# A state-space layer and a gated feed-forward on one Trainium2 core: three steps moved in a hand-ordered kernel

## The chip, the cores and the metric

The kernel runs on one core of one Trainium2 chip. The metric is the device time of one execution in microseconds (us). The time before is the median of five runs: 128.35 us, lowest 126.94, highest 129.66. The profile shown here was taken from one execution of its own.

A core has a matrix engine (TensorE, PE in the profile; PEld is its weight load), a vector engine (VectorE, DVE), an activation engine (ScalarE, ACT), a general engine (GpSimd, POOL) and a queue engine (SyncE, SP) that issues most transfers. Matrix products land in PSUM, in banks; DVE and ACT read PSUM, POOL works on SBUF only.

## The reference

Two layers follow each other. The first is a chunked linear recurrence (a state-space layer) over 4 batches, 8 heads and 768 tokens, with head size 32 and state size 16. The second is a feed-forward with a gate, on 3072 tokens of width 256.

```python
# attention-like layer, per chunk of 32 tokens
cum = np.cumsum(log(a))                       # per head
L   = exp(cum_i - cum_j), causal
M   = (C @ B.T) * L
y   = M @ x + (C @ state) * exp(cum)
state = exp(sum(log a)) * state + sum_j (B_j x_j) * exp(cum_last - cum_j)
# feed-forward
gate = np.maximum(y @ w_gate, 0.0)            # 256 -> 1536
val  = y @ w_val                              # 256 -> 1536
out  = (gate * val) @ w_out                   # 1536 -> 256
```

## The kernel before

**Tiles.** The 3072 tokens are worked in 12 pairs of 256 tokens (pairs 0 to 11, three to a batch) and in 6 blocks of 512 tokens for the feed-forward. Block b takes pairs 2b and 2b+1. `yT` holds the first layer's result, turned, as 128 partitions by 2 halves (k) by 3072 tokens.

**One pair of the first layer** goes through these steps:

- `load(p)`: B, C and x come from memory, six transfers on SP's queue for pairs 4 and later (lines 120 and 121).
- `scale(p, ...)`: POOL multiplies B and C by decay factors into a token tile `tok` (line 333, four operations), issues the transposing transfer `turn_dma` on SP's queue (line 294, the result is `turned`), and casts x into `xb` (line 348). It stands in the queue of POOL and in that of SP where it is called.
- `G`: eight small products of `turned` into four banks (line 540). `gevac`: ACT copies two of the banks (lines 559, 562), POOL blanks their upper triangle (`causal`, line 548), DVE does the others (lines 565, 567).
- `sums`: products of `tok` and `xb` give the state sums (line 593); `states` spreads them on DVE (line 606); `inter` multiplies the carried state with `turned` (line 624).
- `Dm`: sixteen products of the masked `gs` with `xb` (line 635); `yevac` copies the result to `yT` (line 648).

Pairs 0 to 3 have forms of their own ("wide"): `gcopy` and `gmask` for the masks (lines 432, 428), `adds`, `carry` (DVE, line 472) and `pass_on` (ACT, line 481) for the states, `inter_wide` and `D_wide` (lines 493, 518), and `yevac_wide`, whose two halves go to ACT and DVE (line 532).

**The feed-forward of a block** has 12 slices f. `gv(b, f)` makes gate and value for 512 tokens (lines 660, 663), ACT takes the positive part (line 666) and DVE multiplies (line 667) into `h`. `gvh(b, f, u)` does the same for half the tokens (u = 0 or 1; lines 678, 681, 684), so that the first pair of a block can start before the second is ready. With `later=True` it returns the DVE product as a function (`finish`), to be called where the program wants it. `fout` and `foevac` make the block's output and copy it out (lines 705, 721 and others); the transfer out is issued on SP's queue.

**Order.** There is no planner. The order on each engine is the order in which the program writes its steps, and `in_order` at the end keeps it. What waits is decided by semaphores between the queues. `bank()` hands out five shared PSUM banks in turn, so a product into a bank also waits until the bank's last reader is done.

Of the kernel before, what the change touches and what calls it, by code (L numbers as in the profile page):

```python
# [29 lines left out]
def kernel(  # L30
# [13 lines left out]
    nc = tc.nc  # L44
# [8 lines left out]
    NPAIR = T // 256  # L53
# [12 lines left out]
    def bank(name="bank", shape=(128, 512), dtype=FP32):  # L66
        return mm.tile(list(shape), dtype, tag="shared", bufs=NSHARED, name=name)
# [204 lines left out]
    def inverse(b0, b1):  # L272
        for b in range(b0, b1):
            nc.vector.reciprocal(scaleBC[:, b, :, 0, :], scaleBC[:, b, :, 1, :])
# [4 lines left out]
    def scale(p, eng, ceng):  # L279
        scale_bc(p, eng)  # L280
        cast_x(p, ceng)
# [142 lines left out]
    def gmask(p, q, eng, psum=False):  # L424
        s = st[p]
        d = s["gw"][:, q]
        m = (wmask if p < FIRST else wmask3).unsqueeze(2).to_broadcast([128, 2, 2, 128])
        eng.tensor_tensor(out=d, in0=s["gp"][q] if psum else d, in1=m, op=ALU.mult)  # L428
# [47 lines left out]
    def pass_on(p, i):  # L476

        c = 2 * p + i
        S[c + 1] = m = att.tile([128, 2, D], BF16, tag="Sw", name="Sw", bufs=3)
        src = st[p]["A"][i] if c == 0 else T_[c]  # L480
        nc.scalar.mul(m.rearrange("s t d -> s (t d)"), src, dec[:, c:c + 1])
# [28 lines left out]
    def D_wide(p, qs=(0, 1, 2, 3)):  # L510
        s = st[p]
        for t in range(2):
            for r in range(2):
                for i in range(2):
                    half = slice(64 * i, 64 * i + 64)
                    y = s["yw"][i][:, 0:256].rearrange("s (t m) -> s t m", t=2)
                    for q in qs:
                        nc.tensor.matmul(
                            out=y[32 * q:32 * q + 32, t],
                            lhsT=s["xb"][half, 4 * t + q, r], rhs=s["gw"][half, q, r, t],  # L520
                            start=not s["begun"][i] and t == 0 and r == 0, stop=True,
                            tile_position=(64 * i, 32 * q), skip_group_check=True)

    def yevac_wide(p, *engs):
        s = st[p]
        for i, eng in enumerate(engs):
            dst = yT[:, :, p * 256 + i * 128:p * 256 + (i + 1) * 128]
            src = s["yw"][i][:, 0:256].rearrange("s (t m) -> s t m", t=2)
            if p >= FIRST:
                dst = dst.rearrange("s t (m r) -> s t r m", r=2)  # L530
                src = src.rearrange("s t (r m) -> s t r m", r=2)
            (eng.copy if eng is nc.scalar else eng.tensor_copy)(out=dst, in_=src)  # L532
# [158 lines left out]
    def fout(b, ts, fs=range(NF)):  # L691
        if fs[0] == 0 and (ts % 2 == 0 or b == NBLK - 1):
            fst["o"] = bank("o", (128, 2, DM))
        o = fst["o"]
        if b == NBLK - 1 and ts == 3:
            fst["oh"] = [o[:, 1, 0:128], bank("o", (128, 128))]
            for i, oh in enumerate(fst["oh"]):
                for f in range(NF):
                    nc.tensor.matmul(
                        out=oh, lhsT=fst[b][:, f, ts * 128:(ts + 1) * 128],  # L700
                        rhs=wo[:, f, i * 128:(i + 1) * 128], start=(f == 0),
                        stop=(f == NF - 1), skip_group_check=True)
            return
        for f in fs:
            nc.tensor.matmul(  # L705
                out=o[:, ts % 2], lhsT=fst[b][:, f, ts * 128:(ts + 1) * 128],
                rhs=wo[:, f], start=(f == 0), stop=(f == NF - 1),
                skip_group_check=True)

    def foevac(b, ts):  # L710
        last = b == NBLK - 1
        if ts % 2 == 0 and not last:
            if ts and not b:
                fst["ob"] = ob = ffn.tile([128, 2, DM], FP32, tag="ob", name="ob", bufs=3)
                nc.scalar.copy(out=ob[:, 0], in_=fst["o"][:, 0])
            return
        if 1 <= b <= 3:
            if ts == 1:
                fst["ob4"] = ffn.tile([128, 4, DM], FP32, tag="ob4", name="ob4")
            ob = fst["ob4"]  # L720
            nc.scalar.copy(out=ob[:, ts - 1:ts + 1], in_=fst["o"])
            if ts == 3:
                nc.sync.dma_start(
                    out=out[b * 512:(b + 1) * 512, :].rearrange("(i p) m -> p i m", p=128),
                    in_=ob)
            return
        ob = fst.pop("ob", None) or ffn.tile([128, 2, DM], FP32, tag="ob", name="ob", bufs=3)
        r0 = b * 512 + ts * 128
        if last and ts == 3:
            for i, (eng, q) in enumerate(((nc.scalar.copy, nc.scalar),  # L730
                                          (nc.vector.tensor_copy, nc.sync))):
                cs = slice(i * 128, (i + 1) * 128)
                eng(out=ob[:, 1, cs], in_=fst["oh"][i])
                q.dma_start(out=out[r0:r0 + 128, cs], in_=ob[:, 1, cs])
            return
        if last:
            i = ts % 2
            (nc.vector.tensor_copy if i else nc.scalar.copy)(out=ob[:, i], in_=fst["o"][:, i])
            (nc.sync if i else nc.scalar).dma_start(out=out[r0:r0 + 128, :], in_=ob[:, i])
            return  # L740
        if b == 0 and ts == 3:
            nc.scalar.copy(out=ob[:, 1], in_=fst["o"][:, 1])
        else:
            nc.scalar.copy(out=ob, in_=fst["o"])
        nc.sync.dma_start(
            out=out[r0 - 128:r0 + 128, :].rearrange("(i p) m -> p i m", p=128), in_=ob)
# [6 lines left out]
    V, A_, P_ = nc.vector, nc.scalar, nc.gpsimd  # L753
# [54 lines left out]
    def halves(b, u, *fs):  # L808
        for f in fs:
            gvh(b, f, u)  # L810
# [14 lines left out]
    late = [gvh(0, f, 0, True) for f in (1, 2, 3)]  # L825
# [52 lines left out]
    gcopy(2, 1)  # L878
    gmask(2, 3, V, True)
    gmask(2, 0, V)  # L880
    gmask(2, 1, V)
    fout(0, 1)
    foevac(0, 1)
    adds(2)
    carry(2, 0)
    pass_on(2, 0)
    fout(0, 2)
    foevac(0, 2)
    inter_wide(2)
# [10 lines left out]
    gmask(3, 3, V, True)  # L900
    states(3)
    gmask(3, 1, V)
    halves(1, 0, 0, 1, 2, 3, 4)
    y_wide(3)
    inter_full(3, 1)
    D_wide(3)
    yevac_wide(3, A_, V)
    halves(1, 0, 5)

    for b in range(1, NBLK):  # L910
        P, Q, W = 2 * b + 2, 2 * b + 3, 2 * b + 1
        more = P < NPAIR
        for n in (P + 2, P + 3):
            if n < NPAIR and b > 1:
                load(n)

        def at(name, *fs):

            return more and f == fs[min(b, len(fs) - 1)]

        n = 6 if b == 1 else 4
        if b > 1:
            for f in range(n):
                gvh(b, f, 0)
                if f == 1:
                    inter(W, 0)
                    inter(W, 1)
                    Dm(W)
                    if more:
                        sums(P)  # L930
                    yevac(W, nc.scalar)
                    if more:
                        states(P)
        for f in range(n):
            gvh(b, f, 1)
        for f in range(n, NF):
            gv(b, f)
            if b == 1 and at("scale P", 99, 6):
                scale(P, nc.gpsimd, nc.gpsimd)
                load(P + 2)  # L940
                inverse(2, 4)
            if at("scale Q", 9, 6, 4):
                scale(Q, nc.gpsimd, nc.gpsimd)
                if b == 1:
                    load(P + 3)
            if at("scale next P", 11, 11, 9) and P + 2 < NPAIR:
                scale(P + 2, nc.gpsimd, nc.gpsimd)
        if more:
            inter(P, 0)
            if b > 1:  # L950
                inter(P, 1)
        fout(b, 0)
        foevac(b, 0)
        if more:
            G(P)
            if b == 1:
                sums(P)
            gevac(P)
            if b == 1:
                states(P)  # L960
        fout(b, 1)
        foevac(b, 1)
        fout(b, 2)
        foevac(b, 2)
        if more:
            if b == 1:
                inter(P, 1)
            Dm(P)
            sums(Q)
            yevac(P, nc.scalar)  # L970
            G(Q)
            gevac(Q)
            states(Q)
        fout(b, 3)
        foevac(b, 3)

    in_order(tc)

# [29 lines left out]
```

## Time and profile before

| | |
|---|---|
| time, median of 5 runs | 128.35 us (126.94 to 129.66) |
| the profiled execution | 126.94 us |
| its span, first to last instruction | 125.2 us |
| PE busy | 117.8 us (94%) |
| DVE busy | 88.3 us (71%) |
| ACT busy | 76.3 us (61%) |
| POOL busy | 47.9 us (38%) |
| mean granted TensorE clock | 0.997 |

The span leaves 1.74 us of the profiled execution's time outside it. Busy shares are means over the whole span and say little on one stage. Where an engine stood still, and who released it, is read from its waits and its rows in order of time. A row of the timeline gives start, duration, engine, line, operation, tiles and count, and in brackets the idle time before it with the releaser. `SPq` rows are the time that SP took to issue a transfer; when the data had arrived is told by the DMA view ("us to landing", counted from the issue).

### The profile page before, as it was taken

The page shows a single profiled execution, that of the slowest core. Times are in us where ns is not written, and L with a number is a line of the kernel's source. Part 1 is how long each engine was busy: PE and PEld are TensorE (multiplying, and loading weights), DVE is VectorE, ACT ScalarE, POOL GpSimd, SP SyncE. Part 2 cuts the span into 40 slices and gives each one's busy share as a digit, 9 for nine tenths or more (in the row PEclk, how much of TensorE's full clock was granted, in tenths as well). Part 3 has the DMA queues.
Part 4 walks back from the last instruction along what each step waited for, and adds up shares of the span by engine and source line. Part 5 has one row for each costly group of instructions (what it writes and reads, how often), then busy time and mean ns, then how long its engine had stood idle before and what let it go on. Part 6 is the DMA issues. An engine that isn't in the chain of part 4 may idle for free.

```text
span 125.2 us, 3656 instructions
## 1 busy us (share of the span) xinstructions
PE 117.8 (94%) x1398; PEld 82.4 (66%) x1404; DVE 88.3 (71%) x199; ACT 76.3 (61%) x168; POOL 47.9 (38%) x108
## 2 busy tenths in 40 slices
PE   6989999999969996999999999999999999999990
PEld 6766784576756476784467874477864677844790
DVE  4798989771969963698854987845997855687510
ACT  0558598755948631687634786736786545876420
POOL 6499918980364217450333712311800033000000
PEclk9999999999999999999999999999999999999998
DMA  3999999967899999895998099993390002200022
GB/s 66 224 197 141 168 185 196 181 125 102 95 122 185 177 115 110 106 255 72 119 114 166 31 218 113 110 88 86 135 100 0 0 0 89 84 0 0 0 89 84
DMA packets 77489, 13.93 MB, mean 111 GB/s; under 512 B 70064, under 2 KB 77472, under 8 KB 77472
## 3 DMA queue, kind: packets, MB, share of 16 engines
q1 hardware_dynamic: 70128, 10.61, 55.0%
q0 software_dynamic: 4288, 2.36, 14.0%
q10 hardware_dynamic: 3056, 0.72, 2.6%
q8 instruction: 11, 0.18, 0.6%
q14 instruction: 6, 0.05, 0.1%
HBM read 11.13 MB, written 3.15 MB: 114 GB/s over the span
## 4 chain that ended last, share of the span: by engine, by line
PE 68%; SPq 11%; DMA 8%; POOL 6%; issue 2%; DVE 1%; ACT 0%; POOLq 0%; DVEq 0%
PE o L705 17%; PE gv L678 16%; PE val L663 12%; PE gate L660 11%; SPq L120 6%; DMA xr<-in_x_dram 6%; SPq L121 3%; PE y L635 2%; DMA bcr<-in_C_dram 2%; PE w L184 2%; SPq L89 2%; POOL wg L194 2%; PE g L540 2%; POOL bs L317 1%; PE y L624 1%
## 5 line engine op out<-in xcount | busy, mean ns | idle before, releaser
L667 DVE TENSOR_TENSOR h<-r,val 128x512 bf16<-128x512 bf16 x44 | 30.0, 685 | 7.3 <-ACT r L666 7.2
L705 PE MATMUL o<-wo,h 128*128 128x256 bf16 x276 | 33.1, 273 | 0.0
L666 ACT ACTIVATE r<-gate 128x512 bf16<-128x512 f32 x44 | 26.3, 597 | 9.7 <-PE gate L660 9.3
L705 PEld LDWEIGHTS <-h 128*128 128x128 bf16 x276 | 25.9, 98 | 5.3 <-issue 1.7
L663 PE MATMUL val<-yT,wv 128*128 128x512 bf16 x88 | 26.2, 379 | 0.3
L684 DVE TENSOR_TENSOR h<-r,gv 128x256 bf16<-128x256 bf16 x56 | 22.7, 419 | 3.6 <-ACT r L681 2.8
L660 PE MATMUL gate<-yT,wg 128*128 128x512 bf16 x82 | 24.9, 379 | 0.0
L681 ACT ACTIVATE r<-gv 128x256 bf16<-128x256 f32 x56 | 21.2, 385 | 3.6 <-PE gv L678 1.6
L678 PE MATMUL gv<-yT,wg 128*128 128x256 bf16 x112 | 21.6, 273 | 1.3 <-DVE yT L532 1.3
L678 PE MATMUL gv<-yT,wv 128*128 128x256 bf16 x112 | 21.4, 273 | 0.0
L333 POOL TENSOR_TENSOR tok<-bcr,scaleBC 128x128 bf16<-128x128 f32 x32 | 12.1, 402 | 20.7 <-DMA bcr<-in_B_dram 18.7
L565 DVE TENSOR_TENSOR gs<-g,maskUT 128x512 bf16<-128x512 f32 x16 | 10.3, 686 | 12.6 <-issue 5.2
L548 POOL TENSOR_SCALAR_AFFINE_SELECT gs<-gs 128x512 bf16<-128x512 bf16 (+1 forms) x16 | 7.9, 520 | 27.3 <-ACT gs L559 27.3
L663 PEld LDWEIGHTS <-wv 128*128 128x128 bf16 x88 | 8.6, 98 | 10.4
L660 PEld LDWEIGHTS <-wg 128*128 128x128 bf16 x88 | 8.5, 98 | 8.9
L678 PEld LDWEIGHTS <-wg 128*128 128x128 bf16 x112 | 10.3, 98 | 3.1 <-DVE yT L532 1.5
L678 PEld LDWEIGHTS <-wv 128*128 128x128 bf16 x112 | 11.0, 98 | 1.3
L559 ACT CAST gs<-g 128x512 bf16<-128x512 f32 x8 | 4.7, 589 | 6.7 <-PE g L540 6.7
L648 ACT CAST yT<-y 128x512 bf16<-128x512 f32 x8 | 4.7, 585 | 6.4 <-PE A_ps L593 3.7
L428 DVE TENSOR_TENSOR gs<-g,wmask 128x512 bf16<-128x512 f32 x9 | 5.9, 681 | 2.6 <-PE g L413 2.6
L184 PE MATMUL w<-warm 128*128 128x128 bf16 x49 | 5.3, 276 | 1.1 <-DVE tmask L158 1.1
L184 PEld LDWEIGHTS <-warm 128*128 128x128 bf16 x58 | 4.8, 123 | 1.7 <-DVE tmask L158 1.1
(121 smaller groups left out, 116.1 us busy)
## 6 DMA issues: line engine op xcount, KB each, us to landing
xr<-in_x_dram SPq DMA_DIRECT2D x17, 128.0 KB, 3.2
out_dram<-ob SPq DMA_DIRECT2D x3, 512.0 KB, 4.8
bcr<-in_C_dram SPq DMA_DIRECT2D x17, 64.0 KB, 2.9
bcr<-in_B_dram SPq DMA_DIRECT2D x17, 64.0 KB, 3.1
out_dram<-ob SPq DMA_DIRECT2D x4, 256.0 KB, 2.4
xr<-in_x_dram SPq DMA_DIRECT2D x3, 256.0 KB, 3.9
wo<-in_moe_w_out_dram POOLq DMA_DIRECT2D x2, 384.0 KB, 9.1
wg<-in_moe_w_gate_dram POOLq DMA_DIRECT2D x4, 128.0 KB, 4.4
```

Of the source, the lines that this page charges most:

```text
L184: nc.tensor.matmul(out=w, lhsT=warm, rhs=rhs, start=True, stop=True)
L333: eng.tensor_tensor(out=dst[:, t, j * (1 + t)], in0=src[:, j, :, t], in1=f[:, j, :, 4 * t:4 * t + 4].to_broadcast([128, 2, 4, N]), op=ALU. ...
L548: nc.gpsimd.affine_select(out=dst, in_=dst, pattern=[[0, n], [1, 128]], compare_op=ALU.is_ge, fill=0.0, base=0, channel_multiplier=-1)
L565: nc.vector.tensor_tensor(out=d[:, q], in0=g[q], in1=m, op=ALU.mult)
L660: nc.tensor.matmul(out=g, lhsT=wg[:, k, fs], rhs=yT[:, k, tk], start=(k == 0), stop=(k == 1))
L663: nc.tensor.matmul(out=v, lhsT=wv[:, k, fs], rhs=yT[:, k, tk], start=(k == 0), stop=(k == 1))
L666: nc.scalar.activation(r, g, AF.Relu)
L667: nc.vector.tensor_tensor(out=fst[b][:, f], in0=r, in1=v, op=ALU.mult)
L678: nc.tensor.matmul(out=gv_[:, j], lhsT=w[:, k, fs], rhs=yT[:, k, tk], start=(k == 0), stop=(k == 1), skip_group_check=True)
L681: nc.scalar.activation(r, gv_[:, 0], AF.Relu)
L684: nc.vector.tensor_tensor(out=fst[b][:, f, u * 256:(u + 1) * 256], in0=r, in1=gv_[:, 1], op=ALU.mult)
L705: nc.tensor.matmul(out=o[:, ts % 2], lhsT=fst[b][:, f, ts * 128:(ts + 1) * 128], rhs=wo[:, f], start=(f == 0), stop=(f == NF - 1), skip_gr ...
```

## The change

Three steps are moved; nothing is added to or taken from the computation, and the matrix engine's list of instructions keeps its order.

```diff
     gmask(2, 0, V)
-    gmask(2, 1, V)
     fout(0, 1)
-    foevac(0, 1)
     adds(2)
     carry(2, 0)
     pass_on(2, 0)
+    foevac(0, 1)
+    gmask(2, 1, V)
     fout(0, 2)
...
     gmask(3, 1, V)
-    halves(1, 0, 0, 1, 2, 3, 4)
+    late = [gvh(1, f, 0, True) for f in range(5)]
+    late[0]()
     y_wide(3)
     inter_full(3, 1)
     D_wide(3)
+    late[1]()
     yevac_wide(3, A_, V)
+    for fin in late[2:]:
+        fin()
     halves(1, 0, 5)
...
-            if at("scale next P", 11, 11, 9) and P + 2 < NPAIR:
+            if at("scale next P", 99, 99, 9) and P + 2 < NPAIR:
                 scale(P + 2, nc.gpsimd, nc.gpsimd)
...
         fout(b, 3)
         foevac(b, 3)
+        if b == 1:
+            scale(P + 2, nc.gpsimd, nc.gpsimd)
```

- Pair 2: on DVE `carry` goes ahead of the mask of bank 1; on ACT `pass_on` goes ahead of the copy of `fout(0, 1)`.
- Pair 3: DVE's half of `yevac_wide` comes after two of the first five half-tile products instead of after all five.
- Pair 6: in block 1 (P = 4) its `scale` moves from slice f = 11 to the end of the block. On POOL it is now behind the four `causal` operations of pairs 4 and 5; on SP its transposing transfer is now behind block 1's transfer out.

## The prediction

> **What bounds the kernel now.** I first read the totals and the chain that ended last, then the waits of PE.
>
> ```profile
> PE 117.8 (94%) x1398; PEld 82.4 (66%) x1404; DVE 88.3 (71%) x199; ACT 76.3 (61%) x168; POOL 47.9 (38%) x108
> PE 68%; SPq 11%; DMA 8%; POOL 6%; issue 2%; DVE 1%; ACT 0%; POOLq 0%; DVEq 0%
> ...
> PE gv L678 <- DVE yT L532: 1.3, 1, 1.3
> PE y L635 <- POOL gs L548: 1.0, 1, 1.0
> ```
>
> PE sets the time, yet the chain has 11% in SP's issuing and 8% in transfers: between 21 and 49 us it runs along SP's queue. After the start PE has two stalls worth naming, the last two lines, and the change aims at both. Since PE keeps its order, the question is who is next to hold it once they are gone. For that I read the rows in order of time.
>
> First place, 33 to 44 us:
>
> ```profile
> 33.55 1.73 DVE L684 TENSOR_TENSOR h<-r,gv 128x256 bf16<-128x256 bf16 x5
> 35.20 0.43 DVE L532 CAST yT<-y 128x256 bf16<-128x256 f32 x1
> ...
> 34.22 0.44 ACT L532 CAST yT<-y 128x256 bf16<-128x256 f32 x1
> ...
> 35.69 0.28 PE L678 MATMUL gv<-yT,wg 128*128 128x256 bf16 x1 [1.33 <-DVE yT L532]
> ...
> 39.62 1.28 SPq L294 DMA_TRANSPOSE turned<-tok  x1
> ...
> 43.68 0.25 PEld L624 LDWEIGHTS <-Sm 128*128 128x128 bf16 x2 [0.18 <-DMA turned<-tok]
> 43.83 0.28 PE L624 MATMUL y<-turned,Sm 128*128 128x128 bf16 x2
> ```
>
> PE waits 1.33 us for DVE's half of pair 3, which stands behind five products. Eight us later the weight load of `inter(4, 0)` waits 0.18 us for the transposed pair 4: that transfer lands just as PE comes.
>
> Second place, 48 to 54 us (the first two rows are the same work on pair 4, standing for its undisturbed length):
>
> ```profile
> 34.84 1.48 POOL L333 TENSOR_TENSOR tok<-bcr,scaleBC 128x128 bf16<-128x128 f32 x4 [1.50 <-DMA bcr<-in_B_dram]
> 36.26 0.61 POOL L348 CAST xb<-xr 128x512 bf16<-128x512 f32 x1
> ...
> 48.65 0.61 POOL L348 CAST xb<-xr 128x512 bf16<-128x512 f32 x1 [0.65 <-DMA xr<-in_x_dram]
> 49.22 1.00 POOL L548 TENSOR_SCALAR_AFFINE_SELECT gs<-gs 128x512 bf16<-128x512 bf16 x2
> 49.91 0.65 PE L635 MATMUL y<-gs,xb 128*32 128x128 bf16 x16 [0.95 <-POOL gs L548]
> 50.55 0.40 PE L540 MATMUL g<-turned 32*128 32x256 bf16 x8
> 51.74 0.99 POOL L548 TENSOR_SCALAR_AFFINE_SELECT gs<-gs 128x512 bf16<-128x512 bf16 x2 [1.53 <-ACT gs L559]
> 53.62 0.26 PE L593 MATMUL A_ps<-xb,tok 128*32 128x64 bf16 x12
> ```
>
> POOL holds pair 4's blanking back until pair 6's x has come and is cast; `Dm(4)` waits. Then pair 5, and at 53.62 `sums(6)`, the first reader of what `scale(6)` makes. In this execution `scale(6)` was done at 49.26, 4.4 us ahead.
>
> **The change, part by part.** All times are on the axis of the profiled execution: span 125.2 us, 1.74 around it, 126.94 in all. That is 1.41 under the median, so the difference found is carried to the median of 128.35.
>
> *Pair 2's carry.* DVE does the two remaining masks in 1.00 us from 26.93, the carry from 27.85 (0.27); ACT passes the state on from 28.16 (0.35), and PE takes it at 28.54. One mask less ahead (about 0.46) brings the state to about 28.05. But PE comes at 28.54 behind the twelve products of `fout(0, 2)` (27.13 to 28.61), so the gain is between 0 and the 0.2 us that its weight load waited for ACT; I take 0. The mask that moves back ends near 28.2, and `D_wide(2)` starts at 28.87: 0.6 us of cover. The output copy on ACT moves from 27.06 to about 28.1; its transfer is issued only at 38.44, behind a backlog on SP. If either cover failed it would cost its shortfall, some tenths, which part two's idle time on PE would swallow.
>
> *Pair 3's evacuation.* The last mask ends at 33.62. The five products take 1.73, so with 0.42 each they follow at (1.73 − 0.42)/4 = 0.33. Two end at 34.30. PE's `D_wide(3)` ends at 34.15, and on pair 2 DVE's copy began 0.13 after that end (29.29 to 29.42); so it starts at 34.30 and ends at 34.73 by its own 0.43. ACT's half ends at 34.66. Release took 0.06 before (35.63 to 35.69): PE resumes at 34.79, not 35.69. Saved: 0.90. The three products left end at 34.73 + 1.04 = 35.8; PE needs the banks they free from 35.5 on, one each 0.44 us, in order, and the first of them is free at 35.1. So DVE makes no new wait.
>
> PE then reaches `inter(4, 0)` at 42.9, and there stands the transposed pair 4. Its issue starts at 39.62, and the DMA view gives for it:
>
> ```profile
> turned<-tok SPq DMA_TRANSPOSE x1, 4.0
> ```
>
> It lands at 43.62. The weight load follows at 43.68 whatever PE did before. SP is busy without a break from 28.7 to 45.5 with loads that nothing moved here, so the issue at 39.62 stays. The 0.90 us become idle time between 42.9 and 43.8: kept, 0 to 0.9; I take 0, because two views (the wait and the landing) agree within 0.1.
>
> The Trainium skill, page "Perfetto Trace Analysis", section "Summary: the profiler window per engine type", states that for a transfer issued in hardware the shown window ends with the issue and hides the data movement. The issue row here is 1.28 us and the landing 4.0. By the row taken as the transfer's end (40.90) the 0.90 would be kept and the sum would be about 126.1; by the landing it would not. The trace's own landing decides, and it speaks against this edit.
>
> *Pair 6's scale.* Without it POOL blanks pair 4 as soon as ACT's two copies are there (45.77 and 46.25, ending 46.63): done by about 47.4. `Dm(4)` can follow `inter(4, 1)` at 48.79. Sixteen products take 0.33 and the eight of `sums(5)` 0.1, so `G(5)` could start at 49.24, against 50.55: saved 1.31. `G(5)` needs the transposed pair 5, issued at 45.56, 3.7 to landing: 49.26, plus about 0.14 as above for pair 4: 49.40. So 1.15.
>
> Now the work moved is late. From `G(5)` to POOL's start on pair 5 it was 51.74 − 50.55 = 1.19; ACT's copy of pair 4 stands between as before, block 2 shows 1.08. I take 1.12: POOL starts at 50.52, ends 51.51, scales pair 6 from 51.56 (four operations, 1.48) and casts; from the first scaling to the end of the cast pair 4 took 36.87 − 34.84 = 2.03. Done at 53.59, and PE has it at about 53.65. Undelayed, PE would be at `sums(6)` at 53.62 − 1.15 = 52.47. New stall: 1.18. Of 1.15 saved, nothing is left: `sums(6)` at 53.65 against 53.62. What stands behind it on PE is all of block 2; ACT and DVE only wait with it.
>
> The transposing transfer of pair 6 was issued at 52.22, ahead of block 1's output at 53.67. Now the output, copied by about 51.8, goes at 52.17 when the loads of pair 7 are out (0.53), and the transposition waits for POOL's fourth scaling, 53.04. It takes 1.35, so the loads of pairs 8 and 9 start near 54.4, not 54.25. Pair 6's own landing has cover: its reader `inter(6, 1)` comes at 63.5. But behind those loads stands the transposition of pair 7:
>
> ```profile
> 64.94 2.55 SPq L294 DMA_TRANSPOSE turned<-tok  x2
> ...
> 68.37 0.12 PEld L540 LDWEIGHTS <-turned 32*128 32x128 bf16 x8
> ```
>
> 3.2 to landing: 68.14, and PE needs it at 68.37. So 0.2 us of cover, against 0.15 to 0.2 of delay. Even if PE ran a full 2 us earlier up to here, it would wait for this one. Cost 0 to 0.2, taken as 0.05.
>
> **Sum**: 0 − 0 (1.15 − 1.18) + 0.03 + 0.05: about +0.1 us. 127.0 for the profiled execution, 128.4 on the median.
>
> **The rivals.** *Both gains hold*: 0.90 + 1.31 = 2.2, so 126.1. It needs the transposed pairs 4, 5 and 7 to land 0.9 to 2 us sooner and pair 6's scaling hidden. For it: both stalls are real and end where I say. Against it: three landings within 0.3 us of PE's arrival, and 2.03 us of POOL work in front of `sums(6)`.
>
> *Part is kept*: SP's issues vary (0.57 to 2.06 us for loads of the same size), so the chain of landings may stand 0.5 to 1 us better against PE in most executions than in this one. Then about half survives: 0.9, so 127.4. Against it: the profiled execution was the fastest of those shown.
>
> *Slower*: one mechanism, at `G(5)`. It now hangs on pair 5's transposition, and the whole chain `G(5)`, ACT, POOL's blanking, scaling, cast, `sums(6)` (53.65 − 49.40 = 4.25 us) hangs behind it, with nothing left of the former 4.4 us lead. Each tenth by which the landing passes 49.26 is then lost. Landings of the nine transpositions take 2.8 to 5.1; at 5.1 it costs 1.4, less what the old order would also lose (50.66 + 0.14 − 50.55 = 0.25): 1.15 to 1.4, so 129.7. Against it: this transfer took 3.7 here with an unusually long issue (2.03).
>
> *It doesn't do what it says*: the slice after pair 3 could wait for ACT's half instead. That ends at 34.66, no later than DVE's, and the time goes to pair 4's landing anyway: 128.4 too, inside the forecast.
>
> **How the numbers follow.** Forecast 0.60, part kept 0.14, both gains 0.10, slower 0.16. One per cent, 1.28 us, is about what a measurement of this kernel can tell from no change. Faster by over that: 0.10 and 0.05 of the part kept, 0.15. Slower: 0.16. Within: 0.69. The forecast's own bounds (0.2 of gain at pair 2, 0.9 at pair 4's landing cut by the landing of pair 7 to at most 0.3; 0.2 of loss) with the scatter of a median of runs from 126.94 to 129.66 give 127.7 to 129.0. Reaching to the other cases until 2 in 10 are out: 126.9 to 129.7.
>
> **What would show it.** Right: DVE's L532 at about 34.3, PE at `gv` resuming near 34.8, then a wait of about 0.9 for `turned` at L624 near 43.7; no wait of L635 on POOL's L548; a new wait of about 1.2 at L593 on POOL near 53.6; the same start of `G(7)`, 68.4. Wrong: no wait at L624 near 43, L593 at `sums(6)` not waiting, or the chain of transposed pairs landing earlier than here; then time is saved and the rivals above give how much.

## The result and the profile after

The changed kernel takes 127.5 us (median of 43 runs, 126.55 to 128.55); the kernel before, in the runs beside it, 128.07 us (80 runs, 126.01 to 130.63). The ratio is 0.9991, 95% interval 0.9973 to 1.0009: no difference. The forecast was no change, at 128.4 us. (Ratios in this document leave out executions more than 1.5% above the fastest of the same kernel, here 45 of the 80 before and 4 of the 43 after; over all of them the means are 128.24 and 127.51 us, 0.6% apart.) So the change moves the time by less than 1%; whether it gains some tenths of a microsecond stays open.

The page's chain of work that ended last, and PE's waits behind the start (line waited for: us in total, times, longest), both of the changed kernel. Here and below, waits of the first microseconds and waits of 0.2 us or less are left out of such lists:

```profile
PE 76%; POOL 6%; DVE 6%; DMA 5%; SPq 2%; issue 2%; ACT 1%; DVEq 0%
...
PE A_ps L593 <- POOL xb L348: 0.9, 1, 0.9
PE y L624 <- DMA turned<-tok: 0.5, 1, 0.5
PE g L540 <- DMA turned<-tok: 0.5, 1, 0.5
PE gv L678 <- DVE yT L532: 0.4, 1, 0.4
```

Two waits of 1.3 and 1.0 us have become four of 0.4 to 0.9. One is what is left of the first; three are new. The rows in order of time say where each sits:

```profile
34.28 0.45 DVE L532 CAST yT<-y 128x256 bf16<-128x256 f32 x1
34.79 0.28 PE L678 MATMUL gv<-yT,wg 128*128 128x256 bf16 x1 [0.42 <-DVE yT L532]
...
39.83 1.28 SPq L294 DMA_TRANSPOSE turned<-tok  x1
43.56 0.11 PEld L624 LDWEIGHTS <-Sm 128*128 128x128 bf16 x2 [0.97 <-DMA turned<-tok]
...
48.62 0.41 PE L635 MATMUL y<-gs,xb 128*32 128x128 bf16 x16
49.55 0.40 PE L540 MATMUL g<-turned 32*128 32x256 bf16 x8 [0.46 <-DMA turned<-tok]
51.65 1.48 POOL L333 TENSOR_TENSOR tok<-bcr,scaleBC 128x128 bf16<-128x128 f32 x4
53.08 0.60 POOL L348 CAST xb<-xr 128x512 bf16<-128x512 f32 x1
53.73 0.27 PE L593 MATMUL A_ps<-xb,tok 128*32 128x64 bf16 x12 [0.93 <-POOL xb L348]
...
68.50 0.40 PE L540 MATMUL g<-turned 32*128 32x256 bf16 x8
```

The two profiled executions are alike up to pair 3 (`sums(3)` at 30.99 in both), so their times can be set side by side:

| | before | after | gained so far |
|---|---|---|---|
| PE resumes behind pair 3, L678 | 35.69 | 34.79 | 0.90 |
| `inter(4, 0)`, L624 | 43.83 | 43.56 | 0.27 |
| `G(5)`, L540 | 50.55 | 49.55 | 1.00 |
| `sums(6)`, L593 | 53.62 | 53.73 | −0.11 |
| span | 125.2 | 125.4 | −0.2 |

In this pair of executions each gain is made and handed back one station on: the first at the transposed pair 4, the second partly at the transposed pair 5 and the rest at POOL's scaling of pair 6.

### The profile page after: what moved, and what is told of

The parts are those of the page before. It is cut to its first block, busy times and chain, and to the rows that moved or that the text cites. A ratio compares the mean times of both kernels' runs of the same rounds, so it can differ in the third digit from the quotient of the medians.

```text
span 125.4 us, 3658 instructions
## 1 busy us (share of the span) xinstructions
PE 118.2 (94%) x1398; PEld 82.8 (66%) x1404; DVE 88.1 (70%) x199; ACT 76.3 (61%) x168; POOL 48.1 (38%) x108
## 4 chain that ended last, share of the span: by engine, by line
PE 76%; POOL 6%; DVE 6%; DMA 5%; SPq 2%; issue 2%; ACT 1%; DVEq 0%
PE o L705 22%; PE gv L678 16%; PE val L663 14%; PE gate L660 12%; DMA turned<-tok 3%; DVE h L684 3%; DMA bcr<-in_C_dram 2%; PE w L184 2%; POOL wg L194 2%; PE g L540 2%; PE y L635 2%; DVE gs L428 1%; POOL bs L317 1%; PE y L624 1%; POOL tok L333 1%
## 5 line engine op out<-in xcount | busy, mean ns | idle before, releaser
L678 PE MATMUL gv<-yT,wg 128*128 128x256 bf16 x112 | 21.6, 273 | 0.4 <-DVE yT L532 0.4
L678 PE MATMUL gv<-yT,wv 128*128 128x256 bf16 x112 | 21.4, 273 | 0.0
L678 PEld LDWEIGHTS <-wv 128*128 128x128 bf16 x112 | 11.0, 98 | 1.3
L678 PEld LDWEIGHTS <-wg 128*128 128x128 bf16 x112 | 10.3, 98 | 2.2 <-DVE yT L532 0.6
L184 PE MATMUL w<-warm 128*128 128x128 bf16 x49 | 5.8, 293 | 1.1 <-DVE tmask L158 1.1
L606 DVE TENSOR_TENSOR Sm<-A_ps,smask 128x256 bf16<-128x256 f32 x15 | 5.7, 416 | 0.9 <-PE A_ps L593 0.9
```

The lines of the kernel that those rows point to most:

```text
L184: nc.tensor.matmul(out=w, lhsT=warm, rhs=rhs, start=True, stop=True)
L678: nc.tensor.matmul(out=gv_[:, j], lhsT=w[:, k, fs], rhs=yT[:, k, tk], start=(k == 0), stop=(k == 1), skip_group_check=True)
```

## The experiments

The theory: three landings on SP's queue (the transposed pairs 4, 5, 7) and POOL's chain to `sums(6)` take the time. Each of these is called a gate, a thing that PE must wait for once it comes earlier; a gate's cover is the time by which it is ready before PE needs it. Rivals: the edits lose against each other; a single taker; the throughput of the transfers. Every ratio is to the kernel before, run on the same chip in the same job.

**One edit alone.** `e1_pair3` has only pair 3's part of the change's diff, `e2_pair6` only pair 6's.

> The kernel before with pair 3's edit alone. Theory (landings of the transposed pairs and POOL's chain take both gains): PE's wait at L678 falls from 1.33 to about 0.4 us, L624 waits about 0.5 to 0.9 for the transposed pair 4, L635 still waits 0.95 on POOL; ratio to before 1.000. Rival (the gain is real and only pair 6's edit lost it): 0.9 us faster, ratio 0.993.

> The kernel before with pair 6's scale alone moved to the end of block 1. Theory: L635's wait on POOL is gone, L540 waits about 0.5 us for the transposed pair 5, L593 waits 0.9 to 1.2 us on POOL's cast; ratio 1.000. Rival (this edit gains by itself): 1.2 us faster, ratio 0.990. Rival (this edit loses what pair 3's wins): 0.9 us slower, 1.007.

Measured: `e1_pair3` 0.997 (0.9929 to 1.0011), `e2_pair6` 0.998 (0.9945 to 1.0015). PE's waits, first of `e1_pair3`, then of `e2_pair6`:

```profile
PE y L635 <- POOL gs L548: 1.9, 1, 1.9
PE y L624 <- DMA turned<-tok: 1.7, 1, 1.7
PE gv L678 <- DVE yT L532: 0.4, 1, 0.4
```

```profile
PE gv L678 <- DVE yT L532: 1.3, 1, 1.3
PE g L540 <- DMA turned<-tok: 1.0, 2, 0.7
PE A_ps L593 <- POOL xb L348: 0.9, 1, 0.9
```

Each edit takes away the wait that it aims at (L678's falls from 1.3 to 0.4 us, L635's is gone), and for neither is a gain shown, so they don't spoil each other: the second rules out both of its rivals by its interval. The first interval reaches just to the rival's 0.993, so there the trace must speak: L624 waits for the transposed pair 4 as expected. (The profiled execution of `e1_pair3` took 130.95 us at a granted clock of 0.986; its waits are read for who holds whom, not for their size.)

**POOL's chain relieved.** `e4_mid` is the changed kernel with this:

```diff
             if b == 1:
                 states(P)
+                scale(P + 2, nc.gpsimd, nc.gpsimd)
...
-        if b == 1:
-            scale(P + 2, nc.gpsimd, nc.gpsimd)
```

> The changed kernel, with pair 6's scale put on POOL between the blanking of pair 4 and of pair 5. Theory: L593's wait at sums(6) is gone, PE is about 1.0 us earlier from 53 us on, and loses 0.7 to 0.9 of it at G(7), L540, near 68 us, to the landing of the transposed pair 7; ratio to before 0.998. Rival (POOL's chain alone took the gain, no third gate): ratio 0.991.

Measured 0.9961 (0.992 to 1.0001). The rows of PE in `e4_mid`:

```profile
50.53 0.40 PE L540 MATMUL g<-turned 32*128 32x256 bf16 x8 [0.54 <-DMA turned<-tok]
...
53.61 0.26 PE L593 MATMUL A_ps<-xb,tok 128*32 128x64 bf16 x12
...
69.19 0.40 PE L540 MATMUL g<-turned 32*128 32x256 bf16 x8 [0.76 <-DMA turned<-tok]
```

From `G(5)` to `sums(6)` it now takes 53.61 − 50.53 = 3.08 us, against 4.18 in the changed kernel. (This execution had lost time at the transposed pair 4, 1.04 us of wait, so the start times themselves can't be compared.) `sums(6)` no longer waits, and `G(7)` does, 0.76 us, for the transposed pair 7: the third gate that the prediction named stands behind the second. The rival of a single taker (0.991) lies just outside the interval, which rests on five of twelve executions.

`e6b_mid_t7` takes that gate away too: in blocks 2 and 3 the second load is issued behind the transposed pair.

```diff
-        for n in (P + 2, P + 3):
-            if n < NPAIR and b > 1:
-                load(n)
+        if P + 2 < NPAIR and b > 1:
+            load(P + 2)
...
                 scale(Q, nc.gpsimd, nc.gpsimd)
-                if b == 1:
+                if P + 3 < NPAIR:
                     load(P + 3)
```

> The changed kernel with pair 6's scale put on POOL between the blanking of pairs 4 and 5 (as in e4_mid), and in blocks 2 and 3 the second load (pairs 9 and 11) issued after the transposed pair 7 (9) instead of ahead of it. Theory: no wait at L593 for pair 6 nor at L540 for pair 7, the 1.0 to 1.1 us are kept to the end; ratio to before 0.992. Rival (a later gate or the throughput of the transfers): 0.996 to 0.998 as e4_mid.

Measured 0.9878 (0.9805 to 0.9951). The rows of PE in its trace:

```profile
54.38 0.26 PE L593 MATMUL A_ps<-xb,tok 128*32 128x64 bf16 x12
...
69.14 0.40 PE L540 MATMUL g<-turned 32*128 32x256 bf16 x8
```

Neither L593 nor `G(7)` waits; the transposed pairs 4 and 5 still hold PE, 1.27 and 0.41 us. The interval holds the 0.992 expected, but it rests on four of six executions. Over all six, each at a granted clock of 0.997 or more, the ratio of the means is 0.991, by an estimate from their scatter within 0.982 to 0.999: a gain, with the rival's 0.996 not ruled out by time. That the third gate is gone the trace shows.

**SP's queue shortened.** `e5_t4` is the changed kernel with block 0's two transfers out issued at the start of block 4 (`foevac` puts them into a list, the loop over blocks issues the list at b = 4). They stood directly ahead of the transposed pair 4, 1.04 us of issue. `e11_before_out` is the kernel before with this and nothing else.

> The changed kernel, with block 0's two transfers out (1.04 us of SP's issue time, ahead of the transposed pair 4) issued at the start of block 4 instead. Theory (SP's issue queue paces it from 28 to 65 us): pairs 4, 5 and 7 land about 1 us earlier, L624's wait is 0 to 0.1, sums(6) and G(7) come about 0.9 us earlier; ratio to before 0.993. Rival (the DMA engines' throughput paces it): the landings do not move, ratio 1.000.

> The kernel before with block 0's two transfers out issued at the start of block 4, and none of the three edits. Theory (SP's queue paces both kernels from 28 to 65 us): pair 6's x and the transposed pairs land about 1 us earlier, L635 waits less; ratio to before 0.991 to 0.994. Rival (only the changed order can use it): 1.000.

Measured: `e5_t4` 0.9885 (0.9844 to 0.9926), `e11_before_out` 0.9862 (0.9797 to 0.9927). PE's waits, first of `e5_t4`, then of `e11_before_out`:

```profile
PE A_ps L593 <- POOL xb L348: 0.9, 1, 0.9
PE gv L678 <- DVE yT L532: 0.4, 1, 0.4
PE g L540 <- DMA turned<-tok: 0.4, 1, 0.4
```

```profile
PE g L540 <- DMA turned<-tok: 1.4, 2, 0.8
PE gv L678 <- DVE yT L532: 1.3, 1, 1.3
```

In `e5_t4` L624 is gone from the list: the transposed pair 4 was issued at 39.66, which is 4.40 behind PE's return at 35.26, against 39.83 − 34.79 = 5.04 in the changed kernel. From issue to landing it took 3.2 us instead of 3.7. So 0.64 us come with the earlier place in the queue. The other 0.5 may be the throughput: the edit also takes 512 KB of transfers out of this stretch, and no run separates the two. All six executions are faster than the median of the kernel before, and by more than expected (part of why is told with `before2` below).

For the kernel before, the gain is less certain. Its 0.9862 rests on three of six executions. All six ran at a granted clock of 0.998 or more, from 125.99 to 129.08 us, and their mean is 0.993 of that of the kernel before at such a clock, as expected, but by an estimate from their scatter within 0.983 to 1.003. In the trace, of an execution of 128.18 us, L635 is gone from the list, but the transposed pair 5 took 5.8 us to land, and `G(5)` and `G(7)` wait 0.51 and 0.85 us for theirs: from `sums(3)` to `G(7)` it took 38.06 us, against 37.39 in the first profile. So that SP's queue paces the kernel before just as much is not shown.

**The slower rival's mechanism.** `e8b_late5_after` and `e9b_late5_before` put the first three transfers of `load(7)` ahead of the transposed pair 5, in the changed kernel and in the one before:

```diff
+                if b == 1:
+                    load(P + 3, (0,))
                 scale(Q, nc.gpsimd, nc.gpsimd)
                 if b == 1:
-                    load(P + 3)
+                    load(P + 3, (1,))
```

> The changed kernel with the transposed pair 5 issued behind the first three transfers of load(7), some 1.9 us later. Theory (in the changed kernel G(5), POOL's chain and sums(6) hang on this landing with no cover): 1.9 us slower, ratio to before 1.014. Rival (cover is left): under 1.007.

> The kernel before with the same delay of the transposed pair 5. Theory: the old order has about 1.0 us of cover there (landing at 49.26, G(5) at 50.55), so 0.8 to 0.9 us slower, ratio 1.007. Rival (no difference between the orders): 1.014 as e8b_late5_after.

Measured 1.0141 (1.0074 to 1.0207) and 1.0067 (1.0013 to 1.0121). PE's waits (these kernels' lines stand two further down: L542 is `G`, L637 `Dm`), first of `e8b_late5_after`, then of `e9b_late5_before`:

```profile
PE g L542 <- DMA turned<-tok: 3.3, 1, 3.3
```

```profile
PE y L637 <- POOL gs L550: 1.4, 1, 1.4
...
PE g L542 <- DMA turned<-tok: 0.8, 1, 0.8
PE g L415 <- DMA turned<-tok: 0.5, 1, 0.5
PE y L626 <- DMA turned<-tok: 0.4, 1, 0.4
```

The ratios fall where they were expected, but they don't separate the two orders. The intervals overlap, and three of the five executions behind 1.0141 ran at a granted clock of 0.983 to 0.987. At a clock of 1.0 the first kernel took 129.21 and 129.93 us, the second 129.24 in the mean of six: 1.008 and 1.006 of the kernel before. The traces say more. With `sums(3)` at 30.99 in both, `G(5)` comes at 51.70 in `e8b_late5_after` and at 49.55 in the changed kernel, `sums(6)` at 55.88 and 53.73: all 2.15 us are handed on, and since only the order of the transfers differs, the order alone moves this landing. In the kernel before with the same delay, `G(5)` waits 0.80 us for the landing, and the wait on POOL hides the rest. By the traces, then, the change used up the cover; that a late landing therefore costs it more time is not shown by the times.

**All gates moved.** `e7b_all` (`e7_all` in an expectation below is the same kernel) joins `e5_t4` and `e6b_mid_t7`, and issues the transposed pair 5 between the two halves of `load(6)`:

```diff
                 scale(P, nc.gpsimd, nc.gpsimd)
-                load(P + 2)
+                load(P + 2, (0,))
                 inverse(2, 4)
...
                 scale(Q, nc.gpsimd, nc.gpsimd)
+                if b == 1:
+                    load(P + 2, (1,))
```

> All gates moved: the edits of the change; block 0's transfers out at the start of block 4; the transposed pair 5 issued between the two halves of load(6); pair 6's scale between the blanking of pairs 4 and 5; second load of blocks 2 and 3 behind the transposed pair. Theory: the waits at L624, L540, L593 and L635 are all under 0.2 us and both gains hold, 0.9 + 1.3 = 2.2 us less about 0.2: ratio to before 0.984 to 0.986. Rival (bound elsewhere): 0.988 or above, as e5_t4.

Measured 124.8 us, ratio 0.9739 (0.9687 to 0.9791): faster than the kernel before, with no execution as slow as the fastest of either kernel beside the result, and a miss of the expectation on the good side. It was run again beside two others:

> The same as e7b_all, beside the next kernel on one chip: ratio to before 0.974 again, times within 1 us of each other.

> As e7_all with pair 3's edit undone (all five products ahead of DVE's half of the evacuation). Theory (pair 3's edit is worth its 0.9 us once no landing takes it): L678 waits 1.33 us again, no other wait takes it up, 0.9 us slower than e7c_all, ratio to before about 0.981. Rival (DVE's order does not matter to the end): as e7c_all.

> The kernel before once more, for a second profile of it: the first was of an execution faster than the median. If the scatter between executions comes from the landings on SP's queue, an execution nearer the median shows L624 waiting for the transposed pair 4 by more than the 0.2 us of the first profile, and L635 on POOL by more than 0.95. Rival (scatter from the start or from outside the span): the same waits as in the first profile.

Measured: `e7c_all` 124.86 us, 0.9746 (0.9706 to 0.9786); `e10_all_no3` 125.98 us, 0.9825 (0.9784 to 0.9867). The first wait of `gv` in `e7c_all`, then in `e10_all_no3`:

```profile
34.88 0.28 PE L680 MATMUL gv<-yT,wg 128*128 128x256 bf16 x1 [0.42 <-DVE yT L534]
```

```profile
35.78 0.28 PE L680 MATMUL gv<-yT,wg 128*128 128x256 bf16 x1 [1.34 <-DVE yT L534]
```

The two kernels differ in pair 3's edit alone. The waits differ by 0.92 us, the spans are 123.2 and 124.1, and the means of six executions each, all at a granted clock of 0.999 or more, are 125.11 and 126.07 us. So pair 3's edit is worth its 0.9 us, to the end, as soon as no landing takes it. Nothing of this kind was run for pair 6's edit, nor for the parts of the queue's new order one by one: what each of them adds to the 0.974 is not shown.

The miss fits an error in the base better than one in the mechanism. Against the first profile of the kernel before (126.94 us) `e7c_all` is 2.08 us faster, as the sum of 2.2 less 0.2 said. But the ratio goes by other executions of the kernel before, median 128.32 us there, 1.4 us above that profile. The second profile, `before2`, was meant to be nearer the median, but is of one at 131.82 us, slower than any of the 80 beside the result:

```profile
PE y L635 <- POOL gs L548: 1.5, 1, 1.5
PE gv L678 <- DVE yT L532: 1.3, 1, 1.3
...
PE g L413 <- DMA turned<-tok: 0.8, 1, 0.8
PE y L624 <- DMA turned<-tok: 0.6, 1, 0.6
PE g L540 <- DMA turned<-tok: 0.3, 1, 0.3
```

From `sums(3)` to `G(7)` this execution took 73.25 − 34.04 = 39.21, the first profile 68.38 − 30.99 = 37.39. So 1.8 us of the difference lie at the waits on SP's transfers (0.82 at L624, 0.58 at L635, where POOL waits for x, 0.41 at `G(7)`), as expected; but 3.05 us lie ahead of `sums(3)`, of which 0.76 is a wait for the transposed pair 3. Both sides of that expectation are partly right. How much of the 1.4 us this explains in a usual execution is not shown. `e7c_all` keeps its six runs within 0.9 us, the kernel before its nine at a granted clock of 0.997 or more within 1.6; that this comes from the landings alone was not shown.

## Why the prediction was right

The forecast of no change holds by its mechanism, as the list shows. Its figure in microseconds was less good: 127.5 us lies below the forecast's own 127.7 to 129.0, inside the 126.9 to 129.7 that also reaches to the rivals. The base was the median of five runs, 128.35 us; over 80 runs it is 128.07.

- *Pair 2's carry: nothing.* The state was passed on at 27.58 to 27.93 (28.16 to 28.51 before), PE took it at 28.54 in both. Right, the cover too: the moved mask ended at 27.89.
- *Pair 3's evacuation: 0.90.* PE resumed at 34.79, to the hundredth; DVE began at 34.28 (34.30 said).
- *Taken by the transposed pair 4.* Issue at 39.83, 3.7 to landing, 43.5. 0.27 was kept instead of 0, inside the stated 0 to 0.9. The landing was 0.1 earlier than in the first profile; and before, the products came 0.15 behind their weight load (43.68 and 43.83), since PE was still busy, which the forecast left out. `e1_pair3` shows the same wait with this edit alone, `e7c_all` beside `e10_all_no3` the 0.9 us kept once the landing is out of the way.
- *Pair 6's scale: 1.15 gained and 1.18 lost were said, 1.00 and 1.11 came.* `G(5)` at 49.55 (49.40 said), the cast done at 53.68 (53.59), `sums(6)` at 53.73 (53.65). The transposed pair 5 landed at 49.56 and not at 49.26: it was issued 0.1 later and took 3.9 to landing, not 3.7. `G(5)` followed at once, without the 0.14 us that were allowed for it, and so was 0.15 late, the links behind it 0.08 to 0.09.
- *Pair 7's landing.* The loads of pairs 8 and 9 began at 54.48 (54.4 said). They took 10.2 us, not 10.6, so the landing kept its cover (64.74 + 3.3 = 68.0 against 68.50) and cost nothing. As a gate behind the others it is shown by `e4_mid`.
- *Part is kept*, the rival at 127.4 us, is not ruled out as a figure: the changed kernel's median is 127.5, and the means over all executions are 0.7 us apart. Its argument was that the landings stand better against PE in most executions than in the profile. The one other profile of the kernel before shows them standing worse (L624 waits 0.65 us), but it is of an unusually slow execution. So the rival's argument found no support, and whether a part of the gain is kept in a usual execution stays open.

One more thing can be read from the rows and the kernel. The product that waits at L678 reads pair 2's columns of `yT`, copied by 29.85, and not pair 3's. Its first half, k = 0, starts at 34.08 without a wait; only k = 1 waits for DVE's copy of pair 3. In `yT` the half k = 1 of pair 2 lies between the two halves of pair 3, which that copy writes. So the wait of 1.33 us may come from the copy being tracked by its whole stretch of addresses rather than by the columns it writes. No run tests this; a copy for each half would.

## What to carry to other kernels

A stall on the busiest engine is worth no more than the distance to the next thing that holds that engine: before pricing the removal, list for each later step when its inputs land, and take the smallest distance. Where one queue issues nearly all the loads without a break, as here, its order decides when they land: the transposed pair 5, moved behind three loads, brought `G(5)` 2.15 us later. Transfers out that nobody waits for do not belong ahead of one that the busiest engine needs. An edit that gains nothing may still be worth keeping for a later one: here pair 3's edit brought 0.9 us once transfers on SP's queue had changed places.

## What the runs showed of the hardware

In these profiles the transposing transfer of one 128 by 768 tile (bf16, SBUF to SBUF) took 1.2 to 2.8 us of SP's issue time and 2.7 to 5.8 us to land, for the same shape. In the changed kernel the longest landing, 5.5 us, was that of pair 6, issued 0.8 us behind the start of the 512 KB transfer out; in the kernel before, ahead of that transfer, it took 3.0. The other traces don't bear out that this place is the cause: behind the transfer out it took 5.8 (`e2_pair6`), 5.6 (`e5_t4`) and 4.7 (`e8b_late5_after`), ahead of it 3.0 (`e1_pair3`), but also 4.7 (`e4_mid`), 4.8 (`e6b_mid_t7`) and 5.7 (`e11_before_out`).
